# Fixing by hand the instruction order of a kernel's opening, with warm matmuls placed in its gaps

## The chip, the core and the metric

The kernel runs on one core of one Trainium2 chip. The metric is the device time of one execution in microseconds (us); lower is better. The time before was 734.94 us, the median of 4 runs (734.26 to 736.37). Ratios in this text are the mean time of one kernel's fast runs over that of the other's fast runs of the same rounds, so they are not quite the ratio of the medians that are quoted beside them.

The engines are called TensorE (PE in the profile; PEld is its weight load), VectorE (DVE), ScalarE (ACT) and GpSimd (POOL).

## The reference

Two stages follow each other. The first is attention over 4 batches, 8 heads, 768 positions, head size 64; some heads see all earlier positions, the others only 4 sink positions and a window of 64. The second is a mixture of 8 experts on the 3072 resulting rows, with routing weights from 8 rounds of alternate normalizing.

```python
scores = scale * np.matmul(q, k.transpose(0, 1, 3, 2))
scores = np.where(mask, scores, -1e9)            # causal, or causal and (sink or window)
a = exp(scores - max); a = a / (sum(a) + 1e-9)
x = np.matmul(a, v)                              # -> (3072, 512)
P = exp(x @ w_gate - max)
for _ in range(8):                               # rows, then columns
    P /= P.sum(1, keepdims=True) + 1e-9
    P /= P.sum(0, keepdims=True) + 1e-9
    P *= N / E
out = sum(P[:, e:e+1] * (np.maximum(x @ w1[e], 0) @ w2[e]) for e in range(8))
```

## The kernel before

Attention is cut into *units* (batch b, block g of 256 positions, group u of 4 heads) and each unit into *tasks* (two heads, one chunk of keys). Two tasks make a *round*; there are 48 rounds. This is one round's work:

- `emit_prep`: 16 transposes on TensorE (k, then q), then two copies on VectorE out of the matmul accumulator (PSUM) to SBUF;
- `emit_scores`: matmuls of q and k. The closure that it returns, `soften`, is the exponential on ScalarE and the multiply by a mask on VectorE;
- `finish_sums`: the matmuls with v and with ones for the denominators, then Ln and Exp on ScalarE (a reciprocal), then a product on VectorE into `xT`;
- `place_v`: for the first batch, v goes through TensorE and ScalarE into its place;
- `fill`: pieces of expert 0's layers, which give TensorE work between rounds. The first come in round 6.

```python
    keep_warm(blank[:, 0:128], blank, 10)       # 10 matmuls with unused results
    emit_prep(*units[0])
    make_keep()
    make_masks((0, 1))
    # ... (emit_scores and others are defined here)
    for n in range(rounds):
        pair = tasks[2 * n:2 * n + 2]
        for soften in [emit_scores(*t) for t in pair]:
            soften()
        if n % 12 in with_sums:                  # (0, 1, 3, 5, 7, 9, 11)
            if preps:
                emit_prep(*preps.pop())
            if n == 0:
                make_masks((2, 3))
            if n == 1:
                make_far()
            if n in (1, 3, 7):
                place_v((1, 3, 7).index(n))
            finish_sums()
        # ... (the sums of this round are put down for later)
        if n < 6:
            keep_warm(ident16, kTs[units[pair[0][0]]].rearrange("p a s -> p (a s)"), 4)
        if n % 12 == 2 and n > 12:
            emit_logits(n // 12 - 1)
        if quotas[n]:
            fill(-(quotas[n] * (24 - left[0]) // sum(quotas[n:])))
```

Nothing in this text fixes the order in which each engine gets its instructions. The framework's automatic scheduler decides it, from its own simulation of the program. So the program's text and the order in the trace differ, and only the trace shows the latter. Two further facts matter below: the accumulator tiles `sc` (scores, and placed v) and `mo` (transposes, warm matmuls, fill) have two buffers each; and TensorE and VectorE work through their lists in order where the traces show it: in the changed kernel's opening their instructions start in exactly the order of its text (the scores of round 2, whose operands were copied by 16.88 us, started at 17.29, behind six warm matmuls that started at 15.89 to 16.98; VectorE's copy of unit 2's k, transposed by 14.45, started at 16.14, behind two multiplies and a product).

The softmax here doesn't subtract the row's maximum and nothing guards it: scores larger than these inputs give would overflow.

Of the kernel before, what the change touches and what calls it, by code (L numbers as in the profile page):

```python
# [10 lines left out]
F32 = mybir.dt.float32  # L11
# [28 lines left out]
def kernel(  # L40
# [13 lines left out]
    nc = tc.nc  # L54
# [14 lines left out]
    constp = ctx.enter_context(tc.tile_pool(name="constp", bufs=1))  # L69
    xp = ctx.enter_context(tc.tile_pool(name="xp", bufs=1))  # L70
    wp = ctx.enter_context(tc.tile_pool(name="wp", bufs=2))

    nc.scalar.preload_act_table_set("natural_log_exp_and_others")

    NU = 2 * 3 * B
    attn = ExitStack()
# [3 lines left out]
    psA = attn.enter_context(tc.tile_pool(name="psA", bufs=1, space=bass.MemoryType.PSUM))  # L80
# [39 lines left out]
    def place_v(g):  # L120

        t = psA.tile([128, 2, 512], F32, tag="sc", bufs=2, name=f"vp_{g}")
        for n in range(2):
            rows = slice(64 * n, 64 * n + 64)
            for c in range(2):
                nc.tensor.matmul(
                    out=t[64 * c:64 * c + 64, n, :].rearrange("p (h d) -> p h d", h=H),
                    lhsT=ident16[rows, rows], rhs=vraw[g][rows, :, c, :], start=True, stop=True,
                )
        nc.scalar.activation(  # L130
            out=v_tile(0)[:, :, 2 * g:2 * g + 2, :].rearrange("p h n d -> p n h d"),
            in_=t.rearrange("p n (h d) -> p n h d", h=H), func=AF.Copy, bias=0.0, scale=1.0,
        )
# [18 lines left out]
    def load_expert(e):  # L152
        return load_w1(e), load_w2(e)

    expw = {}

    ret_u = constp.tile([128, 2 * H], U32, tag="ret_u")
    nc.sync.dma_start(
        out=ret_u,
# [5 lines left out]
    blank = xT[1][:, 1, NTOK - 512:NTOK]  # L165
    nc.vector.memset(blank, 0.0)
    ident16 = constp.tile([128, 128], F16, tag="ident16")
# [18 lines left out]
    for o in range(2):  # L186
# [3 lines left out]
            out=f4, in_=f4, compare_op=ALU.is_ge, fill=0.0,  # L190
# [22 lines left out]
    def make_keep():  # L213
        nc.vector.scalar_tensor_tensor(
            out=keep[:, 256:512], in0=wm, scalar=1.0, in1=fm, op0=ALU.add, op1=ALU.mult)
        nc.vector.tensor_copy(out=keep[:, 0:256], in_=keep[:, 256:512])
        for rows in sinks:
            nc.vector.tensor_scalar(out=keep[rows, 0:256], in0=fm[rows, :], scalar1=2.0,
                                    scalar2=None, op0=ALU.mult)
        nc.vector.tensor_copy(out=keep[:, 512:640], in_=keep[:, 256:384])  # L220

    def make_masks(js):
        for h in [2 * j + hh for j in js for hh in range(2)]:
            nc.vector.tensor_scalar(
                out=masks[h // 2][:, h % 2, :], in0=keep, scalar1=over[:, h:h + 1],
                scalar2=None, op0=ALU.is_gt,
            )

    def make_far():

        for i in range(2):
            nc.vector.tensor_copy(out=farf[:, :, i], in_=retf)
        for rows in sinks:
            nc.vector.memset(farf[rows, :, 0], 1.0)
        nc.vector.tensor_copy(out=onesf, in_=farf.unsqueeze(3).broadcast_to([128, H, 2, D]))
        nc.vector.memset(ones32, 1.0)
# [7 lines left out]
    def emit_prep(b, g, u):  # L244

        tr = psA.tile([128, 512], F32, tag="mo", bufs=2, name=f"tr_{b}_{g}_{u}").bitcast(F16)
        for i, src in enumerate(kq[b, g]):
            for a in range(2):
                for c in range(2):
                    for hh in range(2):  # L250
                        nc.tensor.transpose(
                            out=tr[64 * hh:64 * hh + 64, ts(4 * i + 2 * a + c, 128)],
                            in_=src[:, 4 * u + 2 * a + hh, c, :], identity=ident16,
                        )
        kTs[b, g, u] = ap.tile([128, 2, 256], F16, tag=f"kT{u}{g}", name=f"kT_{b}_{g}_{u}")
        qTs[b, g, u] = ap.tile([128, 2, 256], F16, tag="qT", bufs=3, name=f"qT_{b}_{g}_{u}")
        for i, dst in enumerate((kTs[b, g, u], qTs[b, g, u])):
            nc.vector.tensor_copy(
                out=dst.rearrange("r a (n c p) -> r a c n p", c=2, p=64),
                in_=tr[:, ts(i, 512)].rearrange("r (a c n p) -> r a c n p", a=2, c=2, p=64),  # L260
            )
# [10 lines left out]
    def keep_warm(lhsT, src, n):  # L272
        for _ in range(n):
            t = psA.tile([128, 512], F32, tag="mo", bufs=2, name="warm")
            nc.tensor.matmul(out=t[:, 0:src.shape[1]], lhsT=lhsT, rhs=src, start=True, stop=True)
# [104 lines left out]
    expw[0] = (expw[0][0], load_w2(0))  # L380
    nc.gpsimd.dma_start(out=wg16, in_=moe_w_gate.rearrange("(c p) e -> p c e", p=128))

    keep_warm(blank[:, 0:128], blank, 10)
    emit_prep(*units[0])
    make_keep()
    make_masks((0, 1))



# [3 lines left out]
    def emit_scores(i, a, ci):  # L393
        b, g, u = units[i]
        if a == 0 and ci == 0:
            if u == 0:
                nb, ng = divmod(3 * b + g + 3, 3)
                if g:
                    emit_vfar(b, g)
                if nb < B:  # L400
                    load_kq(nb, ng)
                    if ng == 1:
                        load_v_heads(nb, 0, 4)
                        load_v_heads(nb, 4, 8)
                elif ng == 0:
                    expw[1] = load_expert(1)
            if i + 1 < len(units):
                preps.append(units[i + 1])
        if ci == 0:
            PTs[i, a] = ap.tile([128, 2, PTW], F16, tag="PT", bufs=4, name=f"PT_{b}_{g}_{u}_{a}")  # L410
        PT = PTs[i, a]
        qT = qTs[b, g, u]
        chunk = chunks_of(g)[ci]
        sc = psA.tile([128, 2, 512], F32, tag="sc", bufs=2, name=f"sc_{i}_{a}_{ci}")
        width = sum(c[2] for c in chunk)
        off = 0
        for kj, qlo, L in chunk:
            for hh in range(2):
                r0 = 64 * hh
                nc.tensor.matmul(  # L420
                    out=sc[:, hh, off:off + L],
                    lhsT=kTs[b, kj // 2, u][r0:r0 + 64, a, ts(kj % 2, 128)],
                    rhs=qT[r0:r0 + 64, a, qlo:qlo + L], start=True, stop=True,
                )
            off += L
        c0 = 512 * ci

        def soften():
            nc.scalar.activation(  # L429
                out=PT[:, :, c0:c0 + width], in_=sc[:, :, 0:width],  # L430
                func=AF.Exp, bias=0.0, scale=SCALE,
            )
            m = masks[2 * u + a]
            if ci == g - 1:
                d = PT[:, :, c0 + 256:c0 + 384]
                nc.vector.tensor_tensor(out=d, in0=d, in1=m[:, :, 384:512], op=ALU.mult)
            if ci == g:
                d = PT[:, :, c0:c0 + 384]
                nc.vector.tensor_tensor(
                    out=d, in0=d, in1=m[:, :, 0:384] if g == 0 else m[:, :, 256:640],  # L440
                    op=ALU.mult)
        return soften

    sums_of = {}
    left = [12 * 8]
# [1 line left out]
    def fill(n):  # L447

        while n > 0 and fillers:
            done = fillers.pop(0)()  # L450
            n -= done
            left[0] -= done

    def finish_sums():
        for (i, a), gen in list(sums_of.items()):
            while run(gen, 1):
                pass
            del sums_of[i, a]
            b, g, u = units[i]
            if (u, a) == (1, 1):  # L460
                one, two = first_steps(b, g)
                at = 4 if (b, g) == (0, 1) else len(fillers)
                fillers[at:at] = one
                fillers.extend(two)
# [3 lines left out]
    quota = {0: 2, 1: 2, 2: 4, 4: 4, 6: 4, 8: 4, 10: 4}  # L468
    rounds = len(tasks) // 2
    quotas = [quota.get(n % 12, 0) if n >= 6 else 0 for n in range(rounds)]  # L470
    for n in range(rounds):
        pair = tasks[2 * n:2 * n + 2]
        for soften in [emit_scores(*t) for t in pair]:
            soften()
        if n % 12 in with_sums:
            if preps:
                emit_prep(*preps.pop())
            if n == 0:
                make_masks((2, 3))
            if n == 1:  # L480
                make_far()
            if n in (1, 3, 7):
                place_v((1, 3, 7).index(n))
            finish_sums()
        for i, a, ci in pair:
            b, g, u = units[i]
            if ci == g:
                sums_of[i, a] = gen_pv(b, g, u, a, PTs.pop((i, a)))
        if n < 6:

            keep_warm(ident16, kTs[units[pair[0][0]]].rearrange("p a s -> p (a s)"), 4)
        if n % 12 == 2 and n > 12:
            emit_logits(n // 12 - 1)
        if quotas[n]:
            fill(-(quotas[n] * (24 - left[0]) // sum(quotas[n:])))
    finish_sums()
    emit_logits(B - 1)
    late[0] = True
# [305 lines left out]
```

## Time and profile before

| what | before |
|---|---|
| median time | 734.94 us |
| first exponential of round 0, 1, 2, 6, 7 on ScalarE | 7.39, 15.47, 20.59, 33.75, 38.62 us |
| half clock in the opening | about 12.2 to 22.4 us |
| first sum of the routing weights (end of attention) | 183.38 us |

The busy line and the clock line of the page of the kernel before. The first gives each engine's busy us, its share of the span and its instructions; the second has 40 equal slices of about 18 us with the granted TensorE clock in tenths.

```profile
PE 708.9 (96%) x7078; PEld 581.7 (79%) x7078; DVE 570.2 (78%) x1115; ACT 427.7 (58%) x794; POOL 161.6 (22%) x198
PEclk8899999999999999999999999999999999999998
```

TensorE is the limit of nearly the whole kernel, and the chain of waits that ended last, which the page follows back over 29% of the span, is nearly all its matmuls. Only the first two slices and the last show a lower clock. The opening is best read engine by engine from the timeline. Its columns are start, duration of the group, engine, source line, operation, output and inputs, shape, count, and in brackets the engine's idle time before it with what ended it.

ScalarE, kernel before (L429 is the exponential, L130 the copy of the placed v):

```profile
7.39 1.51 ACT L429 ACTIVATE PT<-sc 128x768 f16<-128x768 f32 x2 [5.30 <-PE sc L420]
15.47 1.51 ACT L429 ACTIVATE PT<-sc 128x768 f16<-128x768 f32 x2 [6.57 <-PE sc L420]
...
20.59 1.02 ACT L429 ACTIVATE PT<-sc 128x1024 f16<-128x1024 f32 x1 [2.01 <-PE pv L298]
...
33.75 1.95 ACT L429 ACTIVATE PT<-sc 128x1024 f16<-128x1024 f32 x2 [0.87 <-PE sc L420]
38.62 1.73 ACT L429 ACTIVATE PT<-sc 128x768 f16<-128x768 f32 x2 [2.92 <-PE sc L420]
```

Those are rounds 0, 1, 2, 6 and 7. Between rounds 0 and 1 ScalarE waits 6.57 us for scores. VectorE, kernel before (L224 masks, L439 mask multiply, L258 copy of transposed k):

```profile
9.36 1.77 DVE L224 TENSOR_SCALAR mask<-keep,over 128x640 f16<-128x640 f16 x4
11.04 1.01 DVE L439 TENSOR_TENSOR PT<-PT,mask 128x768 f16<-128x768 f16 x2
11.97 0.41 DVE L258 COPY kT<-tr 128x512 f16<-128x512 f16 x1
```

The copies of unit 1, which the scores of round 1 need, stand behind masks and multiplies. TensorE, kernel before (L251 transposes, L420 scores, L298 sums, L341 fill):

```profile
12.90 0.64 PE L251 MATMUL tr<-ident,k 128*64 128x128 f16 x8 [3.08 <-DMA k<-in_k_dram]
14.36 0.64 PE L251 MATMUL tr<-ident,q 128*64 128x128 f16 x8 [0.81 <-DMA q<-in_q_dram]
14.93 0.82 PE L420 MATMUL sc<-qT,kT 64*128 64x256 f16 x8
...
33.31 0.50 PE L420 MATMUL sc<-qT,kT 64*128 64x256 f16 x5
33.74 0.30 PE L298 MATMUL pv<-PT,onesf 128*64 128x256 f16 x2
...
34.25 0.39 PE L420 MATMUL sc<-qT,kT 64*128 64x256 f16 x3
34.57 3.74 PE L341 MATMUL l<-xT,w 128*128 128x256 f16 x32
38.24 0.56 PE L420 MATMUL sc<-qT,kT 64*128 64x256 f16 x8
```

The transposes of unit 2 wait for data, and the scores of round 1 (14.93) stand behind them. The table by stage of the kernel before, in stretches of 3.41 us (columns: stretch, its length, busy us with instruction count of PE, PEld, DVE, ACT, POOL; then the granted clock, DMA share, GB/s):

```profile
8.76:12.17 3.41, 0.95 (x3) 0.10 (x1) 3.38 (x8) 0.14 (x1) 3.41 (x5) 1.00 1.35 131
12.17:15.58 3.41, 1.86 (x24) 1.18 (x24) 2.90 (x7) 0.11 (x1) 3.41 (x5) 0.50 1.59 167
15.58:19.00 3.42, 3.31 (x16) 0.53 (x12) 1.75 (x4) 2.43 (x3) 1.47 (x2) 0.50 1.10 205
19.00:22.41 3.41, 3.41 (x28) 1.62 (x24) 1.20 (x3) 1.82 (x3) 0.00 (x0) 0.50 1.55 191
```

TensorE is busy 0.95 of 3.41 us, and then its clock is a half for three stretches.

### The profile page before, as it was taken

What the parts mean: (1) busy time and instruction counts of PE and PEld (TensorE: products, weight loads), DVE (VectorE), ACT (ScalarE), POOL (GpSimd) and SP (SyncE); (2) the same over time, 40 slices, a digit from 0 to 9 for tenths busy, and PEclk for the clock granted to TensorE, in tenths of its full rate; (3) what the DMA queues carried; (4) which work ended last, traced back from release to release, by engine and by line L of the source; (5) the groups of instructions that cost most, each with busy time, mean ns of one, the idle gap of its engine ahead of it and who ended that gap; (6) DMA issues with size and microseconds to landing.
All of it is one profiled execution on the core that took longest, in us unless ns stands there. A gap on an engine that the chain in (4) does not pass through costs nothing. (4 is left out here: it accounts for less than half of the span.)

```text
span 734.6 us, 17374 instructions
## 1 busy us (share of the span) xinstructions
PE 708.9 (96%) x7078; PEld 581.7 (79%) x7078; DVE 570.2 (78%) x1115; ACT 427.7 (58%) x794; POOL 161.6 (22%) x198
## 2 busy tenths in 40 slices
PE   6999999999999999999999999999999999999994
PEld 2566666766658888888888888888888888888884
DVE  6557465664788998888788878887888788877775
ACT  2766677777488555555555555555555555555551
POOL 8313031000001213121312131213121312121213
PEclk8899999999999999999999999999999999999998
DMA  9999475300073439643964395438642864245876
GB/s 123 189 179 87 46 58 46 30 1 2 1 115 59 73 58 140 106 73 58 140 107 72 58 143 96 79 53 134 103 81 51 138 107 83 49 82 108 151 153 156
DMA packets 83887, 65.88 MB, mean 90 GB/s; under 512 B 50400, under 2 KB 63712, under 8 KB 83808
## 3 DMA queue, kind: packets, MB, share of 16 engines
q0 software_dynamic: 77904, 59.53, 56.7%
q1 hardware_dynamic: 5328, 4.73, 3.0%
q8 instruction: 55, 0.90, 0.5%
q10 hardware_dynamic: 576, 0.52, 0.2%
q14 instruction: 24, 0.20, 0.1%
HBM read 52.45 MB, written 6.29 MB: 80 GB/s over the span
## 5 line engine op out<-in xcount | busy, mean ns | idle before, releaser
L710 POOL DMA_DIRECT2D acc<-add x123 | 103.7, 846 | 389.3 <-ACT add L702 367.8
L626 ACT ACTIVATE R<-l1y 128x512 f32<-128x512 f32 x164 | 98.7, 602 | 126.6 <-PE l1y L617 92.7
L688 PEld LDWEIGHTS <-S 128*128 128x128 f16 x1344 | 131.1, 98 | 16.1 <-issue 0.4
L617 PEld LDWEIGHTS <-S 128*128 128x128 f16 x1312 | 128.0, 98 | 19.5 <-issue 4.3
L705 DVE SCALAR_TENSOR_TENSOR acc<-l2y,Pne,acc 128x256 f32<-128x256 f32 x254 | 110.4, 476 | 30.7 <-PE l2y L688 30.7
L688 PEld LDWEIGHTS <-hT 128*128 128x128 f16 x1008 | 98.5, 98 | 12.1 <-issue 0.6
L429 ACT ACTIVATE PT<-sc 128x1024 f16<-128x1024 f32 (+1 forms) x96 | 84.2, 920 | 39.2 <-PE sc L420 37.0
L617 PEld LDWEIGHTS <-w 128*128 128x128 f16 x984 | 96.1, 98 | 12.2 <-issue 0.6
L617 PE MATMUL l1y<-T,S 128*128 128x256 f16 x656 | 98.4, 273 | 3.2 <-ACT R L626 3.2
L688 PE MATMUL l2y<-T,S 128*128 128x256 f16 x672 | 87.1, 273 | 0.2 <-DVE acc L705 0.2
L702 ACT ACTIVATE add<-l2w,Pne 128x256 f32<-128x256 f32 x82 | 34.5, 473 | 67.5 <-PE l2w L688 67.5
L554 DVE TENSOR_TENSOR S<-hT 128x1024 f16<-128x1024 f16 x84 | 57.7, 686 | 17.2 <-ACT hT L656 14.8
L632 DVE CUSTOM_DVE_ANT_0 hT<-l1z,R 128x512 f16<-128x512 f32 x82 | 56.3, 686 | 9.9 <-ACT R L626 9.8
L632 DVE CUSTOM_DVE_ANT_0 hT<-l1w,R 128x512 f16<-128x512 f32 x82 | 56.2, 685 | 4.4 <-PE l1w L617 0.4
L632 DVE CUSTOM_DVE_ANT_0 hT<-l1y,R 128x512 f16<-128x512 f32 x82 | 55.8, 680 | 0.1
L656 ACT ACTIVATE hT<-l1y 128x512 f16<-128x512 f32 x82 | 49.0, 597 | 1.6
L341 PE MATMUL l<-xT,w 128*128 128x256 f16 x384 | 47.9, 273 | 1.8 <-ACT hT L346 0.7
L626 ACT ACTIVATE R<-l1w 128x512 f32<-128x512 f32 x82 | 49.4, 603 | 0.1
L617 PE MATMUL l1z<-xT,w 128*128 128x256 f16 x328 | 49.4, 273 | 0.0
L617 PE MATMUL l1w<-T,S 128*128 128x256 f16 x328 | 49.4, 273 | 0.0
L617 PE MATMUL l1w<-xT,S 128*128 128x256 f16 x328 | 49.4, 273 | 0.0
L617 PE MATMUL l1y<-T,w 128*128 128x256 f16 x328 | 49.2, 273 | 0.1
(103 smaller groups left out, 1120.4 us busy)
## 6 DMA issues: line engine op xcount, KB each, us to landing
acc<-add POOLq DMA_DIRECT2D x123, 256.0 KB, 3.3
w<-in_moe_w_dram POOLq DMA_DIRECT2D x16, 1024.0 KB, 10.7
out_dram<-acc SPq DMA_DIRECT2D x36, 128.0 KB, 3.0
k<-in_k_dram POOLq DMA_DIRECT2D x11, 256.0 KB, 4.6
q<-in_q_dram POOLq DMA_DIRECT2D x11, 256.0 KB, 5.9
v<-in_v_dram POOLq DMA_DIRECT2D x12, 192.0 KB, 7.6
out_dram<-acc POOLq DMA_DIRECT2D x8, 128.0 KB, 3.4
acc<-in_v_dram POOLq DMA_DIRECT2D x3, 256.0 KB, 6.7
```

Of the source, the lines that this page charges most:

```text
L341: nc.tensor.matmul(out=l1[:, ts(fb % 2, 256)], lhsT=w1[:, dc, ts(fb, 128)], rhs=xT[dc // 2][:, dc % 2, c0:c0 + 256], start=(dc == 0), stop ...
L429: nc.scalar.activation(out=PT[:, :, c0:c0 + width], in_=sc[:, :, 0:width], func=AF.Exp, bias=0.0, scale=SCALE,)
L554: nc.vector.tensor_tensor(out=out_, in0=a_, in1=b_, op=op)
L617: nc.tensor.matmul(out=banks[g, bank][:, f, :], lhsT=lefts1[e][k - 1][:, dc, ts(2 * g + f, 128)], rhs=rights1[c][k - 1][:, dc, :], start=( ...
L626: nc.scalar.activation(out=R[name], in_=banks[g, bank], func=AF.Copy, bias=0.0, scale=1.0)
L632: nc.vector._custom_dve(TENSOR_ADD_SAT, out=block(g, i, n), in0=banks[g, bank], in1=R[name], s0=65504.0, s1=0.0)
L656: nc.scalar.activation(out=block(g, 1, 0), in_=banks[g, "y"], func=AF.Relu, bias=0.0, scale=1.0)
L688: nc.tensor.matmul(out=banks[bank][q], lhsT=lefts2[e, c][k - 1][:, q, f, :], rhs=rights2[e][k - 1][:, f, :], start=(first and (final or q ...
L702: nc.scalar.activation(out=t[:, q, :], in_=banks[bank][q], func=AF.Copy, bias=0.0, scale=w)
L705: nc.vector.scalar_tensor_tensor(out=dst, in0=banks[bank][q], scalar=w, in1=dst, op0=ALU.mult, op1=ALU.add,)
L710: nc.gpsimd.dma_start(out=acc[c][:, i, n, :, :], in_=t, accum_op=ALU.add)
```

## The change

The intent: take the opening (rounds 0 to 5) out of the scheduler's hands. TensorE, VectorE and ScalarE get their instructions there in the order of the text; real work is placed so that no engine stands behind something that waits for a load, and matmuls without use (`idle`, on a block of zeros) go where TensorE would stand still. `soften` is split into its exponential and its mask multiply, so that other work can go between them. Rounds 6 to 47 keep the automatic scheduler. `spend(4)` and `spend(5)` do nothing, as their quotas are zero. The load of the activation table moves a few lines in the text; it starts at 0.81 us in both traces.

```diff
-        def soften():
+        def exp():
             nc.scalar.activation(... func=AF.Exp ...)
+        def mask():
             m = masks[2 * u + a]
             ...
-        return soften
+        return exp, mask
...
-    keep_warm(blank[:, 0:128], blank, 10)
-    emit_prep(*units[0])
-    make_keep()
-    make_masks((0, 1))
...
+    make_far()
+    with tc.manual_schedule(engines={PE, DVE, Activation}):
+        idle(8)
+        emit_prep(*units[0])
+        make_keep()
+        idle(3)
+        r0 = scores(0)
+        emit_prep(*preps.pop())          # unit 1
+        soften(r0, (0,))                 # exponentials only
+        make_masks((0, 1))
+        soften(r0, (1,))                 # mask multiplies only
+        sum_later(0)
+        idle(3)
+        r1 = scores(1)
+        idle(2)
+        soften(r1, (0,))
+        place_v(0)
+        idle(4)
+        make_masks((2, 3))
+        soften(r1, (1,))
+        finish_sums()
+        sum_later(1)
+        emit_prep(*preps.pop())          # unit 2
+        idle(6)
+        r2 = scores(2)
+        soften(r2, (0,)); finish_sums(); soften(r2, (1,)); sum_later(2)
+        emit_prep(*preps.pop())          # unit 3
+        soften(scores(3)); idle(4); place_v(1); idle(3); finish_sums(); sum_later(3)
+        soften(scores(4)); finish_sums(); sum_later(4); spend(4)
+        soften(scores(5)); finish_sums(); sum_later(5); spend(5)
+        emit_prep(*preps.pop())          # unit 4
+    for n in range(6, rounds):           # as before, by the scheduler
...
```

More of the change, by code (lines that the diff above doesn't have):

```diff
@@ L71 @@
     wp = ctx.enter_context(tc.tile_pool(name="wp", bufs=2))
-    nc.scalar.preload_act_table_set("natural_log_exp_and_others")
     NU = 2 * 3 * B
@@ L155 @@
     expw = {}
+    nc.scalar.preload_act_table_set("natural_log_exp_and_others")
     ret_u = constp.tile([128, 2 * H], U32, tag="ret_u")
@@ L470, with spend, sum_later @@
     quotas = [quota.get(n % 12, 0) if n >= 6 else 0 for n in range(rounds)]
-    for n in range(rounds):
-        pair = tasks[2 * n:2 * n + 2]
-        for soften in [emit_scores(*t) for t in pair]:
-            soften()
-        if n % 12 in with_sums:
-            if preps:
-                emit_prep(*preps.pop())
-            if n == 0:
-                make_masks((2, 3))
-            if n == 1:
-                make_far()
-            if n in (1, 3, 7):
-                place_v((1, 3, 7).index(n))
-            finish_sums()
-        for i, a, ci in pair:
+    def spend(n):
+        if quotas[n]:
+            fill(-(quotas[n] * (24 - left[0]) // sum(quotas[n:])))
+    def sum_later(n):
+        for i, a, ci in tasks[2 * n:2 * n + 2]:
             b, g, u = units[i]
@@ L488, with scores, soften, idle @@
                 sums_of[i, a] = gen_pv(b, g, u, a, PTs.pop((i, a)))
-        if n < 6:
-            keep_warm(ident16, kTs[units[pair[0][0]]].rearrange("p a s -> p (a s)"), 4)
+    def scores(n):
+        return [emit_scores(*t) for t in tasks[2 * n:2 * n + 2]]
+    def soften(pairs, which=(0, 1)):
+        for pair in pairs:
+            for w in which:
+                pair[w]()
+    def idle(n):
+        t = psA.tile([128, 512], F32, tag="mo", bufs=2, name="warm")
+        for _ in range(n):
+            nc.tensor.matmul(out=t, lhsT=blank[:, 0:128], rhs=blank, start=True, stop=True)
+    def warm(n):
+        keep_warm(ident16, kTs[units[0]].rearrange("p a s -> p (a s)"), n)
+    engines = {mybir.EngineType.PE, mybir.EngineType.DVE, mybir.EngineType.Activation}
+    make_far()
+    with tc.manual_schedule(engines=engines):
+        idle(8)
[21 more added lines that the diff above has]
+        r2 = scores(2)
+        soften(r2, (0,))
+        finish_sums()
+        soften(r2, (1,))
+        sum_later(2)
+        emit_prep(*preps.pop())
+        soften(scores(3))
+        idle(4)
+        place_v(1)
+        idle(3)
+        finish_sums()
+        sum_later(3)
+        soften(scores(4))
+        finish_sums()
+        sum_later(4)
+        spend(4)
+        soften(scores(5))
+        finish_sums()
+        sum_later(5)
+        spend(5)
+        emit_prep(*preps.pop())
+    for n in range(6, rounds):
+        soften(scores(n))
+        if n % 12 in with_sums:
+            if n == 7:
+                place_v(2)
+            if preps:
+                emit_prep(*preps.pop())
+            finish_sums()
+        sum_later(n)
         if n % 12 == 2 and n > 12:
             emit_logits(n // 12 - 1)
-        if quotas[n]:
-            fill(-(quotas[n] * (24 - left[0]) // sum(quotas[n:])))
+        spend(n)
     finish_sums()
```

## The prediction

(The sum is 33.75 less about 30.2 us at round 6, taken as 3.5 to 4 us off 734.94; 731.0 is at the upper end of that.)

> **What bounds the kernel now.** From about 50 us on, TensorE does: busy 96% of the span (busy table), 19 to 20 us of every 20 between 80 and 160 us (table by stage), and the chain of waits that ended last is TensorE matmuls. The change leaves that work alone. It rewrites the order of the opening only: rounds 0 to 5 of attention, up to the first scores of round 6, which start at 33.31 us (timeline of TensorE).
>
> In that opening no engine is full. The timeline shows three losses.
> 1. The scheduler put the transposes of the second position block (they wait for k until 12.90 and q until 14.36 us) ahead of the scores of round 1. Those scores start at 14.93, although their own transposes were done at 8.2; VectorE copied them only from 11.97 on, behind masks and mask multiplies. ScalarE idles 6.57 us between the exponentials of rounds 0 and 1.
> 2. TensorE is idle from 9.8 to 12.9 us, and the granted clock is 0.50 from about 12.2 to 22.4 us (table by stage). [...]
> 3. Rounds 2 to 5 run on ScalarE from 20.59 to 33.75 us with gaps.
>
> **What changes.** Same real work; 33 warm matmuls instead of 34 (8+3+3+2+4+6+4+3 against 10+24), now placed in the gaps. Copies of unit 1 go ahead of the masks; scores of round 1 ahead of the transposes of unit 2.
>
> My walk through the new order, with durations from the trace:
> - VectorE: keep mask until 9.4, copies of unit 1 until 10.2, four masks (1.8), round 0's multiplies (1.0) until 13, four masks (2.0), round 1's multiplies (1.0) until 16, xT product (0.7), copies of unit 2 (0.8) until about 17.4.
> - So round 1's exponentials start near 10.5 instead of 15.47, but round 2's only near 17.8 instead of 20.59: VectorE, and behind it the landing of q at 14.4, takes 2 us back.
> - ScalarE from round 2 to round 6: eight exponentials 7.4, two ln/exp pairs 2.5, one v copy 1.0, sum 10.9 us, plus about 1.4 where scores of round 4 wait behind sums that need the placed v. Round 6's exponentials then start near 30.2 instead of 33.75.
>
> **How much is critical.** Everything after is TensorE work in the same order, and the weights of expert 0 should be there in time (first use 34.57, no wait on it now). So 3.5 to 4 us should pass to the end nearly undiluted; later rescheduling may add or take 1 us.
>
> **Predicted time: 731.0 us**, range 728.5 to 733.3. Faster by over 2% (14.7 us) is nearly impossible, as the whole opening is 33 us: 0.01. Within 2%: 0.98. Slower: 0.01.
>
> **What would show it.** Right: no half-clock stretch after the opening, or a much shorter one; first exponential of round 1 near 10.5, of round 2 near 17.8, of round 6 near 30; every later stage shifted by the same 3 to 4 us with unchanged length.
>
> **What would make it wrong.** The clock still drops; a warm matmul or a placed v blocks the in-order TensorE queue; earlier loads delay the weights; the automatic scheduler reorders rounds 6 to 47 and gains or loses there; or the opening gains up to 6 us because I overestimate VectorE's chain.

## More of the kernel before

The stretches are 3.41 us long because the clock's records are, in multiples: in this trace 6.83 us at full clock (from 5.34), 10.24 at half and 706.56 at full, which is 2, 3 and 207 times 3.413 us. Only the last record, 7.71 us at half clock at the very end, is no such multiple. Last, VectorE's first sum over the routing weights marks the end of attention, and serves below as one clock hand for all kernels:

```profile
183.38 0.35 DVE L505 TENSOR_REDUCE rs<-Pne 128x24 f32<-128x192 f32 x1 [0.89 <-ACT Pne L326]
```

## The result, and the profile after

| | before | after |
|---|---|---|
| median (range, runs) | 734.69 us (733.50 to 737.07, 16) | 729.63 us (728.71 to 733.78, 11) |
| ratio of the fast runs | | 0.9938, 95% interval 0.9923 to 0.9953 |
| first exponential of round 1, 2, 6, 7 | 15.47, 20.59, 33.75, 38.62 | 10.64, 17.73, 30.59, 33.88 us |
| first sum of the routing weights | 183.38 (second profile 183.94) | 178.63 (second profile 178.28) us |

The medians differ by 5.06 us; the ratio stands for 0.62% of 734.7, or 4.6 us. Both are inside the 2% that counts as "same", as predicted. The busy and clock lines of the page after:

```profile
PE 703.8 (97%) x7077; PEld 581.4 (80%) x7077; DVE 569.7 (78%) x1115; ACT 427.3 (59%) x794; POOL 161.6 (22%) x198
PEclk9999999999999999999999999999999999999999
```

Nothing was removed but one warm matmul. TensorE is busy 5.1 us less. The three half-clock stretches before had 8.6 us of busy time (1.86, 3.31 and 3.41); at full clock that would be about 4.3 us less (an estimate: warm matmuls of 512 columns start 0.427 us apart at half clock, at 21.95 us in the kernel before, and 0.216 us apart at full clock, at 16.12 us in the changed kernel), so most of the difference is matmuls that ran at half speed. ScalarE, after (L426 is the exponential now), rounds 0, 1, 2, 6 and 7:

```profile
7.76 1.51 ACT L426 ACTIVATE PT<-sc 128x768 f16<-128x768 f32 x2 [5.66 <-PE sc L417]
10.64 1.51 ACT L426 ACTIVATE PT<-sc 128x768 f16<-128x768 f32 x2 [1.37 <-PE sc L417]
...
17.73 1.73 ACT L426 ACTIVATE PT<-sc 128x1024 f16<-128x1024 f32 x2 [2.46 <-PE sc L417]
...
30.59 1.94 ACT L426 ACTIVATE PT<-sc 128x1024 f16<-128x1024 f32 x2 [2.04 <-PE sc L417]
33.88 1.73 ACT L426 ACTIVATE PT<-sc 128x768 f16<-128x768 f32 x2 [1.35 <-PE sc L417]
```

The wait before round 1 fell from 6.57 to 1.37 us. But of the 4.83 us won there, 2.86 are left at round 2 and 3.16 at round 6, where ScalarE now waits 2.04 us. At round 7 the lead is 4.74 us. VectorE, after, around unit 2:

```profile
12.81 1.88 DVE L225 TENSOR_SCALAR mask<-keep,over 128x640 f16<-128x640 f16 x4
14.61 1.01 DVE L438 TENSOR_TENSOR PT<-PT,mask 128x768 f16<-128x768 f16 x2
15.54 0.68 DVE L310 TENSOR_TENSOR xT<-pv,rc 128x512 f16<-128x512 f32 x1
16.14 0.41 DVE L259 COPY kT<-tr 128x512 f16<-128x512 f16 x1
```

VectorE works without a wait from 7.58 to 18.08 us now, and the copies of unit 2 are the last of a row. TensorE, after, around round 6 (L342 is the fill):

```profile
28.95 1.05 PE L342 MATMUL l<-xT,w 128*128 128x256 f16 x8
...
30.16 0.61 PE L417 MATMUL sc<-qT,kT 64*128 64x256 f16 x8
30.70 2.86 PE L342 MATMUL l<-xT,w 128*128 128x256 f16 x24
33.50 0.56 PE L417 MATMUL sc<-qT,kT 64*128 64x256 f16 x8
```

Before, all 32 fill matmuls came after the scores of round 6. After, TensorE does 8 of the 32 while the scores wait for their copies. That is how a lead of 3.16 us on ScalarE at round 6 becomes 4.74 us at round 7: the queue behind round 6 is shorter. The 8 fill matmuls are 0.88 us of it (3.74 less 2.86). The other 0.7 us are matmuls of earlier sums (33.74 to 34.25), which stood among the scores of round 6 before and do not after. The table by stage after, again in 3.41 us stretches:

```profile
7.13:10.54 3.41, 2.35 (x35) 1.22 (x35) 2.87 (x9) 1.51 (x2) 3.41 (x6) 1.00 1.12 105
10.54:13.96 3.42, 2.98 (x32) 1.32 (x26) 3.42 (x8) 2.43 (x3) 3.42 (x5) 1.00 1.44 140
13.96:17.37 3.41, 2.25 (x26) 1.09 (x26) 3.41 (x8) 1.23 (x2) 2.23 (x3) 1.00 1.36 193
...
24.20:27.61 3.41, 1.92 (x30) 1.34 (x31) 1.82 (x4) 3.38 (x5) 2.41 (x3) 1.00 1.35 205
```

The clock stays full in this trace and in the second one, from its first record (at 7.13 and 5.04 us) to the last few us, though the last of these stretches has only 1.92 of 3.41 us busy. It may not stay full in every execution. The record lists the mean granted clock of 12 runs of the changed kernel: the four slowest (731.23 to 733.78 us) have 0.993 to 0.995, the other eight (728.71 to 730.36 us) 0.996 to 0.998. In the two traces the half clock at the very end, 3.5 and 5.6 us long, is all that lowers the mean. By an estimate from these means 0.993 over 730 us means about 10 us at half clock; where these lay was not traced. And the end of attention:

```profile
178.63 0.35 DVE L566 TENSOR_REDUCE rs<-Pne 128x24 f32<-128x192 f32 x1 [0.89 <-ACT Pne L327]
```

From round 7 to about 430 us the lead stays flat (4.74 to 4.77 us, instruction by instruction on ScalarE). Yet the spans of this pair of profiles are 734.6 and 727.4 us, 7.2 apart. The rest came late: the first profile of the kernel before lost 0.75 us near 437 us and 0.9 us near 511 us, where the two kernels do the same work in the same order. Its second profile (`before_again`) was 0.56 us behind the first at the end of attention and 0.54 us ahead of it from 530 us on, so such stalls belong to single runs. The span of one pair of profiles would have overstated the gain by 2 us.

### The profile page after: what moved, and what is told of

Read it like the earlier page. It is cut to its first block, busy times and chain, and to the rows that moved or that the text cites. A ratio compares the mean times of both kernels' runs of the same rounds, so it can differ in the third digit from the quotient of the medians.

```text
span 727.4 us, 17373 instructions
## 1 busy us (share of the span) xinstructions
PE 703.8 (97%) x7077; PEld 581.4 (80%) x7077; DVE 569.7 (78%) x1115; ACT 427.3 (59%) x794; POOL 161.6 (22%) x198
## 5 line engine op out<-in xcount | busy, mean ns | idle before, releaser
L678 PEld LDWEIGHTS <-S 128*128 128x128 f16 x1312 | 128.1, 98 | 17.8 <-issue 2.6
L426 ACT ACTIVATE PT<-sc 128x1024 f16<-128x1024 f32 (+1 forms) x96 | 83.8, 919 | 35.2 <-PE sc L417 35.2
L342 PE MATMUL l<-xT,w 128*128 128x256 f16 x384 | 48.1, 273 | 1.7 <-ACT hT L347 0.7
```

Of the source, the lines that this page charges most:

```text
L342: nc.tensor.matmul(out=l1[:, ts(fb % 2, 256)], lhsT=w1[:, dc, ts(fb, 128)], rhs=xT[dc // 2][:, dc % 2, c0:c0 + 256], start=(dc == 0), stop ...
L426: nc.scalar.activation(out=PT[:, :, c0:c0 + width], in_=sc[:, :, 0:width], func=AF.Exp, bias=0.0, scale=SCALE,)
L678: nc.tensor.matmul(out=banks[g, bank][:, f, :], lhsT=lefts1[e][k - 1][:, dc, ts(2 * g + f, 128)], rhs=rights1[c][k - 1][:, dc, :], start=( ...
```

## The experiments

Leads below are read at the first sum of the routing weights, against 183.66 us, the mean of the two profiles of the kernel before. Two profiles of one kernel differed there by 0.56 us (before) and 0.35 us (after), so a lead is good to about 0.4 us. The changed kernel's mean lead is 5.2 us (178.63 and 178.28). The expectations were written with the first pair alone, 4.75 us.

Where the 0.35 us between the two profiles of the changed kernel come from can be read: q of unit 2 landed at 15.50 us in the first and at 14.75 in the second. In the first, six warm matmuls stood behind the late transposes of q and held the scores of round 2 until 17.29 us, 0.4 us after VectorE's copies were done; in the second these scores started with the end of the copies, at 16.95.

| run | median us | ratio to before (95%) | lead us |
|---|---|---|---|
| changed kernel | 729.63 | 0.9938 (0.9923 to 0.9953) | 5.2 |
| x1 old order, warm clock | 732.03 | 0.9975 (0.9958 to 0.9992) | 2.8 |
| x2 new order, no warm matmuls after the first 8 | 731.44 | 0.9958 (0.9943 to 0.9973) | 2.2 |
| x3 late copies of unit 1 | 734.84 | 1.0002 (0.9985 to 1.0019) | 1.0 |
| x5 late copies, warm clock | 732.52 | 0.9969 (0.9953 to 0.9985) | 2.7 |
| x9 x1 with early copies | 731.94 | 0.9952 (0.9935 to 0.9969) | 3.3 |
| x4 unit 4 earlier | 728.72 | 0.9925 (0.9911 to 0.9940) | 6.7 |
| x6 x4, unit 2 copied earlier | 728.54 | 0.9915 (0.9899 to 0.9931) | 8.0 |
| x7 x6, v placed earlier | 727.57 | 0.9902 (0.9887 to 0.9916) | 7.7 |
| x8 x7, fill in rounds 4 and 5 | 732.08 | 0.9959 (0.9945 to 0.9972) | 3.9 |

The kernel before had 734.62 us in the rounds of x1 to x4, 735.22 in those of x5 to x8 and 735.21 in that of x9. All results were correct. The traces show the orders that are told below.

The leads rest on one profile for each run (two for the changed kernel). The times are the mean of several runs, but coarser: by the ratios, with intervals of about 1.2 us to either side, the gain is 1.8 us in x1, 3.1 in x2, 2.3 in x5, 3.5 in x9 and 4.6 in the changed kernel. They agree with the leads within these intervals, except in x4 and x6, where the ratios give 5.5 and 6.2 us and the leads 6.7 and 8.0. By themselves the times do not tell apart parts of 2 or 3 us.

The theories: A, the order gave most of the gain; B, the clock did.

### x1: the clock alone

The old order of TensorE in rounds 0 and 1 was written out by hand, since, by the author's account (no run of it is kept), four or more extra warm matmuls in the plain text made the scheduler reorder it. Then 12 warm matmuls went into the gap. Up to the first placing of v the lists of the engines stayed the same but for one mask multiply on VectorE; from there to round 6 the scheduler exchanged some neighbouring groups on TensorE.

```diff
-            keep_warm(ident16, kTs[units[0]]..., 4)
+            keep_warm(ident16, kTs[units[0]]..., 4 + 12)
```

> The kernel before with its own order, only with 12 more warm matmuls (16 instead of 4) in TensorE's gap that ended at 12.90 us. Theory A (the order on VectorE, ScalarE and TensorE gave most of the gain): the half-clock stretch of 10.2 us goes, but round 2 still waits for the q copy that ended at 17.2, so the first exponential of round 2 moves from 20.59 to about 19 and the end moves by 1 to 2 us at most. Theory B (the clock gave most of it): the end moves by 3.5 us or more, that is most of the 4.75 us by which all work after round 7 is earlier in the changed kernel.

Measured: the clock is 1.00 throughout in the table by stage. Round 1's exponentials start at 15.55 (before 15.47), round 2's at 18.73 (before 20.59), and the lead grows to 2.5 us against the first profile by round 4. It is 2.8 us in the end against the mean of the two profiles (2.5 against the first), between the two expectations: neither theory covers the whole, and the clock is worth about half. The clock is not quite alone in this run: eight of the warm matmuls wait 0.62 us for VectorE's copies of unit 1 (the transposes hold one of the two `mo` buffers until then), and the transposes of unit 2 stand behind them past q's landing at 14.20 us. x9 comes back to this. TensorE, x1:

```profile
12.78 1.89 PE L275 MATMUL warm<-kT,ident 128*128 128x512 f16 x8 [0.62 <-DVE qT L258]
...
15.17 0.50 PE L416 MATMUL sc<-qT,kT 64*128 64x256 f16 x8
```

### x2: the new order without the warm matmuls

```diff
         idle(8)            # kept
-        idle(3) ... idle(3) ... idle(2) ... idle(4) ... idle(6) ... idle(4) ... idle(3)
```

> The changed kernel without its 25 warm matmuls after the first 8; the order of all other instructions is unchanged. Theory A (order): even if the clock falls to a half for about 10 us, the end stays 2.5 us or more ahead of the kernel before. Theory B (clock): the clock falls and 3 us or more of the gain are lost. A third outcome, the clock stays full without the warm matmuls: then the time is the changed kernel's or up to 0.5 us less, because six of them stand in front of the scores of round 2.

The table by stage of x2; the stretch that decides stands ahead of the one that is slow:

```profile
5.42:8.83 3.41, 1.73 (x34) 1.12 (x32) 1.65 (x5) 1.51 (x2) 3.36 (x7) 1.00 1.29 125
8.83:12.25 3.42, 1.12 (x12) 0.64 (x12) 3.39 (x10) 1.16 (x2) 3.42 (x5) 0.50 1.27 119
...
25.90:29.31 3.41, 1.81 (x33) 1.23 (x29) 1.71 (x4) 3.38 (x6) 1.06 (x2) 1.00 1.25 206
29.31:32.73 3.42, 3.42 (x39) 2.53 (x33) 1.44 (x4) 0.50 (x1) 1.56 (x2) 0.50 1.89 178
```

The clock fell twice, for 13.65 and 3.41 us. 2.2 us of lead are left (3.2 by the medians), so the warm matmuls are worth 3.0 us in the new order by the lead. By the medians they are worth 1.8 us. The result lies at the edge of both expectations. Again each half does about half.

The two falls did not cost the same. Against the first profile of the changed kernel, round 4 starts 1.25 us later (25.32 against 24.07), after the long fall, and round 6 starts 2.87 us later (33.46 against 30.59), after the short one. So 13.65 us at half clock cost 1.25 us where TensorE had gaps, and 3.41 us cost 1.6 us where it was busy throughout. And the fall is not certain: of the six timed runs five had a mean clock of 0.985 to 0.987, but one had 0.997, and it was the fastest (730.04 us). There the third outcome of the expectation seems to have come true; that run was not traced.

### x3: late copies of unit 1

```diff
         r0 = scores(0)
-        emit_prep(*preps.pop())
         soften(r0, (0,))
         make_masks((0, 1))
         soften(r0, (1,))
+        emit_prep(*preps.pop())
```

Only VectorE's list changes by this: the two copies move behind four masks and two multiplies.

> The changed kernel with one step undone on VectorE alone: the copies of unit 1 follow the four masks and the multiplies of round 0, as in the kernel before; TensorE's and ScalarE's orders are unchanged. If the early scores of round 1 count (theory A): exponentials of round 1 start near 13.4 instead of 10.64, those of round 2 near 19 instead of 17.73, and the end is 1 to 1.5 us later than the changed kernel's. Rival: round 2 waits only for q, which landed at 15.5, so the start of round 2 moves by under 0.3 us and the end does not move.

Both expectations missed. The loss was 4.2 us of the 5.2 us, and the time was that of the kernel before. The table by stage of x3:

```profile
8.92:12.33 3.41, 0.07 (x1) 0.00 (x0) 3.36 (x9) 0.00 (x0) 3.41 (x5) 1.00 1.34 127
12.33:15.74 3.41, 2.73 (x16) 0.82 (x17) 3.35 (x8) 1.83 (x3) 3.41 (x5) 0.50 1.53 179
```

Late copies let TensorE stand still for a whole stretch, and the clock fell for 6.8 us. An order on VectorE had become a clock on TensorE, and the two had to be separated.

### x5: late copies, with the clock kept

```diff
         sum_later(0)
-        idle(3)
+        idle(20)
         r1 = scores(1)
```

> The run x3 again (copies of unit 1 behind the masks), but TensorE's wait from 9 to 13 us filled with 17 more warm matmuls. x3 lost 4.06 us of the 4.75 us: its clock fell to a half for 6.8 us. If the late copies cost time only through the cold clock: the clock stays full and all after round 7 is within 0.5 us of the changed kernel. If the order costs by itself: round 1's exponentials start near 13.5 as in x3, those of round 2 near 19, and all after round 7 is 1 to 2 us later than in the changed kernel.

ScalarE, x5, rounds 1 and 2:

```profile
13.55 1.51 ACT L426 ACTIVATE PT<-sc 128x768 f16<-128x768 f32 x2 [4.68 <-PE sc L417]
...
20.05 1.73 ACT L426 ACTIVATE PT<-sc 128x1024 f16<-128x1024 f32 x2 [1.87 <-PE sc L417]
```

The clock stayed full and the lead is 2.7 us. So the late copies cost 2.5 us by order alone (5.2 less 2.7), a little more than expected, and in x3 a further 1.7 us by the clock. What is left in x5 is about what the clock alone gave in x1 (2.8). All the other reordering, without these copies, gave nothing that can be seen within the 0.4 us.

### x9: early copies in TensorE's old order

x1, with VectorE's copies of unit 1 ahead of the masks; TensorE's list is the same as in x1.

```diff
+            emit_prep(*preps.pop())      # unit 1
             make_masks((0, 1))
             for soften in first:
                 soften()
-            emit_prep(*preps.pop())
```

> x1 (the old order with a warm clock) with one more change, on VectorE alone: the copies of unit 1 go ahead of the masks, as in the changed kernel. TensorE's order is x1's: the scores of round 1 stay behind the transposes of unit 2, which wait for q until about 14.3. If the early copies are worth their 2.33 us (x5 against the changed kernel) by themselves: all after round 7 is 2 us earlier than in x1. If they are worth it only together with TensorE's new order: round 1's exponentials still start near 15.5 and the end moves by less than 0.7 us against x1.

Round 1's exponentials start at 15.04 us (15.55 in x1), and the lead is 3.3 against 2.8 us. TensorE, x9:

```profile
14.31 0.41 PE L251 MATMUL tr<-ident,q 128*64 128x128 f16 x8 [0.96 <-DMA q<-in_q_dram]
14.66 0.51 PE L416 MATMUL sc<-qT,kT 64*128 64x256 f16 x8
```

The medians are equal (731.94 and 732.03), but they come from different rounds; by the ratios to the kernel before, x9 is 1.7 us faster, with intervals that overlap. So it is the traces that carry the comparison. The same two copies that are worth 2.5 us with the new list of TensorE are worth 0.5 us at most with the old one, where the scores of round 1 stand behind transposes that wait for q (landed at 14.27 us), although their own operands were copied by 10.20 us. And even the 0.5 us are explained by the wait of x1's own warm matmuls: the scores start at 14.66 instead of 15.17, because no warm matmul waits for the copies now and the transposes start as q lands. So x9 may be the cleaner measure of the warm clock alone, and would put it at 3.3 us. For round 1 both lists must change for either to count.

### x4, x6, x7, x8: is there more in the opening?

x4 moves the transposes and copies of unit 4 ahead of the scores of round 5, against ScalarE's wait of 2.04 us.

```diff
+        emit_prep(*preps.pop())
         soften(scores(5))
         finish_sums()
         sum_later(5)
         spend(5)
-        emit_prep(*preps.pop())
```

> The changed kernel with the transposes and copies of unit 4 issued before the scores of round 5 instead of after its sums. In the changed kernel ScalarE idles 2.04 us before round 6, and TensorE is busy only 0.3 to 0.6 of each us from 25 to 28. If this wait is on the critical path: the first exponential of round 6 moves from 30.59 to about 28.6 and the end moves by 1 to 2 us. If TensorE's total work until round 7 is the limit instead, the end moves by less than 0.5 us.

Round 6 starts at 28.58 us, and the lead is 6.7 us, 1.5 more than the changed kernel's. The wait was on the critical path.

x6 puts VectorE's copies of unit 2 ahead of round 1's multiplies.

```diff
         make_masks((2, 3))
+        for gen in sums_of.values():
+            run(gen, 2)                  # only the sums' matmuls
+        emit_prep(*preps.pop())
         soften(r1, (1,))
         finish_sums()
         sum_later(1)
-        emit_prep(*preps.pop())
-        idle(6)
+        idle(4)
```

> x4 with VectorE's copies of unit 2 ahead of round 1's multiplies and the xT product, and two warm matmuls fewer before the scores of round 2. If VectorE's order sets the start of round 2: its exponentials start at about 16 instead of 17.37 and the end is about 1 us ahead of x4. If q's landing (14.2 to 15.5) or ScalarE downstream takes it back: less than 0.3 us at the end.

ScalarE, x6, round 2:

```profile
15.91 1.73 ACT L426 ACTIVATE PT<-sc 128x1024 f16<-128x1024 f32 x2 [0.64 <-PE sc L417]
```

Round 2 starts at 15.91 instead of 17.37 us (x4) and the lead rises by another 1.3 us to 8.0. So VectorE's chain had set the start of round 2 in x4 (there the scores wait 0.83 us for its copy), as the prediction's walk had it, with q's landing (14.12 us in this run) close behind.

x7 places the second part of v before the scores of round 3.

```diff
         emit_prep(*preps.pop())          # unit 3
+        place_v(1)
         soften(scores(3))
         idle(4)
-        place_v(1)
-        idle(3)
         finish_sums()
```

> x6 with the second placing of v ahead of the scores of round 3, so that ScalarE's 0.94 us wait before round 4 goes. If ScalarE is the limit of rounds 2 to 6: the end is 0.6 to 1 us ahead of x6. If TensorE's work is: under 0.3 us.

It missed: the lead is 7.7 against 8.0 us, equal within what two profiles differ by, and ScalarE's wait before round 4 is still 1.01 us. The placed v takes one of the two `sc` buffers, so now half of round 3's scores wait 1.15 us for ScalarE's copy of v, and four warm matmuls stand before the sums. The wait had moved from one engine to another. The median is the lowest of all (727.57 us), but x6 and x7 are not told apart.

x8 adds expert 0's first layer to rounds 4 and 5.

```diff
+    quotas[4] = quotas[5] = 2
```

> x7 with two units of expert 0's first layer each after rounds 4 and 5, so that TensorE does real work in its gaps there. If TensorE has gaps left and the weights have landed (about 21 us): all after about round 8 is 0.5 to 1.5 us earlier than in x7. If the fill only delays the scores that feed ScalarE: no gain or a loss of up to 1 us.

It lost 3.8 us of lead against x7, more than either expectation. TensorE, x8, ahead of round 5, and the exponentials of round 5:

```profile
23.68 1.92 PE L342 MATMUL l<-xT,w 128*128 128x256 f16 x16
26.99 0.41 PE L252 MATMUL tr<-ident,k 128*64 128x128 f16 x8 [1.38 <-DVE hT L349]
...
27.99 1.73 ACT L426 ACTIVATE PT<-sc 128x1024 f16<-128x1024 f32 x2 [2.38 <-PE sc L417]
```

The fill's results take both `mo` buffers, and the transposes of unit 4 behind it wait 1.38 us for VectorE to empty one; ScalarE then waits 2.38 us. Useful work is not free filler when it holds a buffer that the critical work needs. The changed quotas also altered the scheduler's lists from round 6 on, so not all of the 3.8 us is shown to come from this one place.

### before_again and after_again

Both kernels unchanged, one look each.

> The kernel before, unchanged, for a second profile. Its first sum of the routing weights should start within 0.3 us of 183.38, with the same half-clock stretch. If the late part (440 to 530 us), where the first profile fell another 1.65 us behind the changed kernel's, is a matter of the single run, this profile's late part differs from the first by a few tenths of a us to 2 us.

> The changed kernel, unchanged, for a second profile. The lead over the kernel before at the first sum of the routing weights should be 4.75 us again within 0.3 us, and the clock full in the opening again; the lead in the spans is expected to differ from the 7.2 us of the first pair of profiles.

The sums started at 183.94 and 178.28 us, 0.56 and 0.35 us off the first profiles, so both missed the 0.3 us that was expected. The half-clock stretch came again in one (12.86 to 23.1 us) and was absent in the other. The spans were 733.6 and 727.4 us, 6.2 apart.

## Why the prediction was right, and what it mis-sized

The class, the direction and the range held: 731.0 us were predicted (728.5 to 733.3), 729.63 measured. Point by point:

- **TensorE is the limit afterwards, so the shift passes on.** Right. The lead is flat from round 7 to about 430 us. Late differences belonged to single runs.
- **The half clock goes.** Right in both traces of the changed kernel, though that filled gaps keep the clock up was not yet shown then (the trace before had one fall, after a stretch busy for 0.95 of 3.41 us); the mean clock of some of its timed runs hints at a fall. x1 and x9 show the clock's worth in the old order (2.8 to 3.3 us) and x2 in the new one (3.0 us).
- **Round 1 near 10.5, round 2 near 17.8.** Measured 10.64 and 17.73. The prediction's reason, that VectorE's chain takes 2 us back, is shown by x6, which moved the copies of unit 2 and so moved round 2, and by the second profile of the changed kernel, where the scores of round 2 wait for the copies and round 2 starts at 17.38. That the first profile met 17.8 so closely is in part luck: VectorE's copies were done at 16.88, not 17.4, and the warm matmuls behind the late q made up the difference.
- **Round 6 near 30.2, "So 3.5 to 4 us should pass to the end nearly undiluted".** Here the step failed in size. Round 6 started at 30.59, a lead of 3.16 us, yet 4.74 us passed on in that pair of profiles, and 5.06 us by the medians. That 30.2 was nearly met is luck in part: from round 2 to round 6 ScalarE was busy 9.9 us, not 10.9, and waited 3.0 us (0.94 before round 4, 2.04 before round 6), not 1.4. And the walk followed ScalarE only and took its lead for TensorE's. But ScalarE's wait before round 6 was 2.04 us after against 0.87 before, and TensorE used its share of that time for 8 of the 32 fill matmuls (0.88 us); the sums that had stood among the scores of round 6 (0.7 us) were behind it as well. The lead to be carried forward was that of TensorE's queue, read at the scores of round 7 (38.24 against 33.50).
- **Which part gives what.** The prediction named three losses and did not divide the gain. The runs do: 2.8 us for the clock alone (x1), 2.5 us for two copies on VectorE placed early (x5 against the changed kernel); together 5.3, against 5.2 measured. (With x9 for the clock it is 5.8; four leads, each good to 0.4 us, do not decide between the two.) The copies count only with TensorE's new list (x9), and late copies cost the clock as well if nothing fills the gap (x3).
- **The automatic scheduler may gain or lose in rounds 6 to 47.** It put the fill before round 6's scores, which helped, and the flat lead shows that nothing else came of it.

The best version found, x6 or x7, is ahead of both kernels: ratio 0.9915 and 0.9902 to the kernel before, leads 8.0 and 7.7 us. The interval of x7 (0.9887 to 0.9916) lies clear of the changed kernel's (0.9923 to 0.9953); that of x6 (0.9899 to 0.9931) overlaps it. All of this is inside the 2% that counts as "same".

## What to carry to other kernels

Follow the lead on the engine that limits the *later* work, at the first point where its queue is the same in both kernels; the lead of a feeding engine can be smaller or larger. When an order is changed, ask on each engine's list what stands in front of the critical instruction: here a move on one engine was worth 0.5 us at most, and 2.5 us once the other engine's list had moved too. A gap on TensorE cost twice in x3, once as a gap (2.5 us) and once as a slow clock after it (1.7 us), so separate the two by filling the gap with work without use before you say which it was. See that the filler does not itself wait for something: in x1 it held up real work by 0.5 us. And a slow clock cost most where TensorE had no gaps: in x2 1.6 us for 3.41 us of it, against 1.25 us for 13.65 us where there were gaps.

## What the traces show of the clock

- The clock also fell where TensorE was not idle: in x2 after stretches of 3.41 us with TensorE busy for 1.73 and for 1.81 us by the profile (51 and 53%). In the openings of the other runs it held after 1.87 (x3), 1.89 (x5) and 1.92 us (the changed kernel). These are shares of the profile's busy time in stretches that lie differently in each execution (the first record of the clock stands at 5.34 and at 6.04 us in the two profiles of the kernel before).
- In both profiles of the kernel before, a stretch busy for 3.31 and 3.30 of 3.41 us was still followed by a slow one, and only the next, fully busy one ended it; yet in x2 the clock rose after a stretch with 2.94 us. What decides it is not shown.
- The first record of the clock stands at 3.98 to 7.13 us (5.34 in the kernel before), and the table by stage shows 1.00 ahead of it. Yet the first ten warm matmuls of 512 columns in the kernel before started 0.427 us apart, as two of that size did in its recorded half clock (at 21.95 and 22.38 us), and six of the same size at full clock, at 15.89 us in the changed kernel, 0.216 us apart. So the opening began at half clock.
